# FNet mixing and SwiGLU: folding the first batch crosswise, set by set, and fetching its weights behind x

## The chip, the cores and the metric

The kernel runs on one core of a Trainium2 chip. The metric is the device time of one execution in microseconds (us). One execution was also recorded by the hardware profiler. All times below are from those runs and from that profile.

## The reference

`x` has 8 batches of 3008 rows by 256 columns, in float32. Each batch goes through a Fourier transform over rows and one over columns, and the real part is kept. The 24064 rows then go through a SwiGLU block with 1536 hidden columns.

```python
def _attn_ref(x):
    X = np.fft.fft(x, axis=1)
    X = np.fft.fft(X, axis=2)
    return X.real.astype(np.float32)

def _moe_ref(x, w_gate, w_val, w_out):
    g = x @ w_gate
    silu = g * (1.0 / (1.0 + np.exp(-g)))
    val = x @ w_val
    return (silu * val @ w_out).astype(np.float32)
```

## The kernel before

**What is computed where.** The column transform is folded into the weights: `Wp` and `Wq` are the gate and value weights multiplied by tables of cosines (`CD`) and sines (`SDt`), and `Wm` is `Wq` times -2 but for one row. The row transform is a matmul with a table of cosines and sines, `Tab`. Its length is cut by symmetry: the rows of a batch are cut into four quarters of 752 rows; rising rows of a quarter are added to falling rows of another (a sum and a difference), and the columns of the result are folded once more, the upper half reversed onto the lower. What is left are two sets of rows, set A with 128 rows (buffer `XA`) and set C with 60 rows of each half (buffer `XC`; batch 0 uses `XC0`). The matmuls with `Tab` give, for each batch, a sum part and a difference part, from which additions and subtractions on VectorE write the tiles `Pt` and `Qt` of 480 or 512 columns. These are the inputs of the feed-forward part.

**The main loop.** For each tile there are 12 units of 128 hidden columns. A unit is a matmul for the gate and one for the value, from `Pt` with `Wp` and from `Qt` with `Wq` or `Wm` (line 1337); then a Silu on ScalarE (line 1372 in the first units, later 1449, 1472, 1521, 1524), a product on VectorE or GpSimd (1375, 1540, 1548, 1551), and a matmul with `Wo` (line 1601). A planner written in the kernel sets the order in which these and the work for the next batches are issued. The scheduled work of the first tile also holds the transform of the remaining weight columns (lines 1808 to 1823), which come from `Wraw`, and the fetch of `Wo` (line 1974).

**The prologue.** Everything ahead of the main loop is written out by hand, and each engine runs its instructions in the order in which they are written. All of the change lies here.

- Lines 264 to 274: the fetches of x for batch 0. Rising rows of set A come in one DMA, falling ones in four, two of them issued by ScalarE. Set C comes in two rises (`rise_c`, line 270) and four falls (`fall_c`, line 273). Line 277 clears half of `XC0` on ScalarE first. SP's DMAs use eight semaphores in turn, and one that takes a semaphore again waits for the landing of the one that had it.
- Lines 356 to 411: small tables, and `row_signs`, on GpSimd. Line 363 (`turns`) and line 367 (`angles`) make the angles for `Tab`; lines 374, 377, 383 and 386 are the sines, cosines, negated copies and the weighing of `Tab` on ScalarE. `load_w` fetches the first 512 columns of the two weights (line 394, tiles `W0`) and the others (line 396, `Wraw`, which lies in the memory of `XA` and so waits until set A has been read).
- Line 444 (`place`): a matmul with a permutation brings the rising rows into the order of the falling ones.
- Line 453 (`sums`): sums and differences of the placed rows and the falling ones, for set A into `SA` and for set C into `SC`, 128 x 512 each, on VectorE.
- Line 511 (`fold_d`): the columns of set A folded, on GpSimd, into `EOA` in float32; line 512 casts that to `EOb` on ScalarE. Line 507 (`fold_c`) folds set C on VectorE into bfloat16.
- Lines 497 and 503 (`half_folded`, `folded_c`): the matmuls with `Tab`. Line 611 (`row0`): the column 0 that the fold leaves out, as matmuls with one row of output; its operands come from `heads` (lines 457, 458, GpSimd).
- Line 473 (`half_w`): the first weights times `CD` or `SDt`, in halves of 256 columns with gate and value in one PSUM bank; the copies out of PSUM are lines 475 (ScalarE) and 477 (VectorE), and line 481 (`double`) writes `Wm`.
- Line 642 copies the one part of the product to SBUF (`od`), and line 647 (`put`) writes `Pt` and then `Qt` from it on VectorE.
- Line 668: two entries of the operand `BBc` of batch 0 (`St`). Line 669 clears a piece of `Af`, and line 671 is two DMAs of SP that write these zeros into the unused partitions of `XC`. The same queue of SP then holds the loads of batch 1: set C (lines 166, 168, 175), a copy inside `XC` (line 180), and set A (lines 151, 153). The folds of batch 1 run on GpSimd (lines 189 to 213).

Of the kernel before, what the change touches and what calls it, by code (L numbers as in the profile page):

```python
# [17 lines left out]

@with_exitstack
def kernel(
# [27 lines left out]

# [12 lines left out]

# [55 lines left out]

# [147 lines left out]
    nc.scalar.copy(xf[:, 4 * D:8 * D], zero.to_broadcast([P, 4 * D]))  # L277
# [39 lines left out]

# [148 lines left out]

    def half_w(h, k, pool, nm):
        ps = pool.tile([P, 2, T // 2], F32, name=nm)
        dst, tab = ((Wp, CD), (Wq, SDt))[k]
        fs = slice(h * T // 2, (h + 1) * T // 2)  # L470
        for gv in range(2):
            for no in range(2):
                nc.tensor.matmul(ps[:, gv, :], tab[:, no, :], W0[gv][:, no, fs], start=(no == 0), stop=(no == 1))
        if k or not h:
            nc.scalar.copy(dst[:, :, fs], ps)
        else:
            nc.vector.tensor_copy(dst[:, :, fs], ps)

    def double(h):
        fs = slice(h * T // 2, (h + 1) * T // 2)  # L480
        nc.scalar.activation(Wm[:, :, fs], Wq[:, :, fs], AF.Copy, scale=m2)
# [33 lines left out]
    def transform_w(fc, gv, k, ps):  # L515
        dst, tab = ((Wp, CD), (Wq, SDt))[k]
        src = W0[gv] if fc == 0 else Wraw[gv][:, :, (fc - 1) * T:fc * T]
        fs = slice(fc * T, (fc + 1) * T)
        for no in range(2):
            nc.tensor.matmul(ps, tab[:, no, :], src[:, no, :], start=(no == 0), stop=(no == 1))  # L520

        def copies():
            if k:
                nc.scalar.copy(dst[:, gv, fs], ps)
                if fc == 1:
                    nc.scalar.activation(Wm[:, gv, fs], ps, AF.Copy, scale=m2)
                else:
                    pts(Wm[:, gv, fs], dst[:, gv, fs], scalar1=m2, scalar2=1.0, op0=Alu.mult, op1=Alu.mult)
            else:
                nc.vector.tensor_copy(dst[:, gv, fs], ps)  # L530
        return copies

    def first_rows():
        ps = psO.tile([P, T], F32, name="o")
        for gv in range(2):
            for f in range(nF):
                nc.tensor.matmul(ps[:, gv * nF + f:gv * nF + f + 1], Wq[0:1, gv, f * P:(f + 1) * P], sel[0:1, 0:1],
                                 start=True, stop=True)
        nc.scalar.copy(w0.rearrange("p g f -> p (g f)"), ps[:, 0:2 * nF])

# [22 lines left out]
    for k, a in ((0, 0), (1, 0), (0, 1)):  # L563
        sums(SC, k, XC0, psC, (a,))
# [1466 lines left out]
```

## Time and profile before

| | |
|---|---|
| median of 3 runs | 600.81 us (600.59 to 600.97) |
| the profiled execution, span | 599.1 us (1.7 below the median of the runs) |
| TensorE busy | 589.5 us, 98% |
| VectorE busy | 572.4 us, 96% |
| ScalarE busy | 562.6 us, 94% |
| GpSimd busy | 515.5 us, 86% |
| granted TensorE clock from 2 us to 82 us | 1.00 |

In the profile PE is TensorE, PEld its weight loads, DVE VectorE, ACT ScalarE, POOL GpSimd and SP SyncE, which issues DMAs; SPq, POOLq and PEldq are the instructions of an engine's own queue, DMA issues and waits among them. A row of the timeline gives the start, the duration, the engine, the line, what is written from what, the count, and in brackets the idle time of the engine ahead of it with what ended that. A row that stands for several instructions (x2) gives the time from the first start to the last end.

### The profile page before, as it was taken

The page shows a single profiled execution, that of the slowest core. Times are in us where ns is not written, and L with a number is a line of the kernel's source. Part 1 is how long each engine was busy: PE and PEld are TensorE (multiplying, and loading weights), DVE is VectorE, ACT ScalarE, POOL GpSimd, SP SyncE. Part 2 cuts the span into 40 slices and gives each one's busy share as a digit, 9 for nine tenths or more (in the row PEclk, how much of TensorE's full clock was granted, in tenths as well). Part 3 has the DMA queues.
Part 4 walks back from the last instruction along what each step waited for, and adds up shares of the span by engine and source line. Part 5 has one row for each costly group of instructions (what it writes and reads, how often), then busy time and mean ns, then how long its engine had stood idle before and what let it go on. Part 6 is the DMA issues. An engine that isn't in the chain of part 4 may idle for free.

```text
span 599.1 us, 12479 instructions
## 1 busy us (share of the span) xinstructions
PE 589.5 (98%) x3968; PEld 391.7 (65%) x4027; DVE 572.4 (96%) x1058; ACT 562.6 (94%) x1090; POOL 515.5 (86%) x464
## 2 busy tenths in 40 slices
PE   8999999999999999999999999999999999999997
PEld 6556666666666666566666666666666666666676
DVE  8989998999999999999999999999999999999993
ACT  8899999999989999899999999998999999999995
POOL 9828999999799999999999988997899557787772
PEclk9999999999999999999999999999999999999999
DMA  9846347344816314354245112046121211111112
GB/s 243 145 101 138 115 117 189 86 131 117 173 60 138 108 55 126 108 128 140 63 91 149 36 45 82 19 123 166 51 62 37 63 47 54 54 47 46 59 54 80
DMA packets 50556, 57.66 MB, mean 96 GB/s; under 512 B 7268, under 2 KB 37400, under 8 KB 50490
## 3 DMA queue, kind: packets, MB, share of 16 engines
q1 hardware_dynamic: 47449, 53.91, 33.7%
q0 software_dynamic: 2672, 2.36, 2.7%
q8 instruction: 31, 0.51, 0.3%
q10 hardware_dynamic: 368, 0.59, 0.3%
q14 instruction: 36, 0.29, 0.2%
HBM read 29.43 MB, written 24.65 MB: 90 GB/s over the span
## 4 chain that ended last, share of the span: by engine, by line
PE 85%; DVE 5%; ACT 3%; DMA 3%; issue 2%; POOL 2%; SPq 0%; POOLq 0%; ACTq 0%; DVEq 0%
PE o L1601 37%; PE g L1337 23%; PE v L1337 19%; PE g L1760 2%; PE o L1760 2%; DVE sv L1540 2%; DMA XA<-in_x_dram 1%; DMA XA<-in_moe_w_gate_dram 1%; DVE hp L1551 1%; DVE es L1474 1%; ACT sv L1524 1%; PE v L1601 1%; POOL hm L1548 1%; ACT v L1410 1%; PE o L1808 1%
## 5 line engine op out<-in xcount | busy, mean ns | idle before, releaser
L1548 POOL TENSOR_TENSOR hm<-sv 128x1024 bf16<-128x1024 f32 (+2 forms) x137 | 254.9, 1862 | 49.4 <-DVE sv L1540 21.5
L1540 DVE SCALAR_TENSOR_TENSOR sv<-es,v 128x512 f32<-128x512 f32 (+2 forms) x262 | 174.2, 669 | 7.4 <-PE v L1337 5.2
L1601 PE MATMUL o<-Wo,hm 128*128 128x256 bf16 (+1 forms) x1128 | 163.2, 273 | 0.4
L1601 PE MATMUL o<-Wo,hp 128*128 128x256 bf16 (+1 forms) x1104 | 159.3, 272 | 0.5
L1551 DVE TENSOR_TENSOR hp<-sp,v 128x512 bf16<-128x512 f32 (+2 forms) x236 | 157.0, 669 | 2.1 <-PE v L1337 1.4
L1601 PEld LDWEIGHTS <-hm 128*128 128x128 bf16 (+2 forms) x1140 | 111.8, 98 | 57.3 <-issue 1.1
L1601 PEld LDWEIGHTS <-hp 128*128 128x128 bf16 (+2 forms) x1140 | 111.9, 98 | 54.9 <-issue 1.5
L1524 ACT ACTIVATE sv<-g 128x512 f32<-128x512 f32 (+2 forms) x178 | 118.1, 674 | 4.2 <-PE g L1337 2.3
L1449 ACT ACTIVATE sp<-g 128x512 f32<-128x512 f32 (+2 forms) x178 | 111.1, 625 | 4.8 <-PE g L1337 1.3
L1410 ACT ACTIVATE v<-bc,w 128x512 f32<-128x512 bf16 (+2 forms) x147 | 105.7, 721 | 1.0 <-DVE hp L1551 0.6
L1337 PE MATMUL v<-Pt,Wp 128*128 128x512 bf16 (+2 forms) x287 | 106.0, 375 | 0.5
L1337 PE MATMUL g<-Pt,Wp 128*128 128x512 bf16 (+2 forms) x281 | 104.9, 374 | 0.2
L1472 ACT ACTIVATE es<-v 128x512 f32<-128x512 f32 (+2 forms) x147 | 90.7, 622 | 4.3 <-PE v L1337 2.2
L1474 DVE SCALAR_TENSOR_TENSOR es<-bc,w,v 128x512 f32<-128x512 bf16 (+2 forms) x127 | 92.9, 734 | 1.4 <-PE g L1337 0.4
L1337 PE MATMUL g<-Qt,Wq 128*128 128x512 bf16 (+2 forms) x247 | 90.4, 374 | 0.7
L1337 PEld LDWEIGHTS <-Wp 128*128 128x128 bf16 x576 | 56.3, 98 | 27.2 <-issue 0.8
L1337 PE MATMUL g<-Qt,Wm 128*128 128x512 bf16 (+2 forms) x187 | 70.3, 376 | 0.3
L1453 DVE SCALAR_TENSOR_TENSOR sg<-bc,w,g 128x512 f32<-128x512 bf16 (+2 forms) x96 | 69.2, 721 | 0.3 <-PE g L1337 0.2
L1524 ACT ACTIVATE sv<-sg 128x512 f32<-128x512 f32 (+2 forms) x96 | 66.5, 697 | 0.4 <-DVE sg L1517 0.4
L1521 ACT ACTIVATE sp<-g 128x512 f32<-128x512 f32 (+2 forms) x96 | 59.2, 616 | 5.9 <-DVE sg L1517 5.5
L1517 DVE SCALAR_TENSOR_TENSOR sg<-sg,g 128x512 f32<-128x512 f32 (+2 forms) x96 | 63.4, 660 | 0.5
L1337 PEld LDWEIGHTS <-Wq 128*128 128x128 bf16 x429 | 41.9, 98 | 26.9 <-issue 0.7
(196 smaller groups left out, 777.3 us busy)
## 6 DMA issues: line engine op xcount, KB each, us to landing
out_dram<-ev SPq DMA_DIRECT2D x96, 128.0 KB
XA<-in_x_dram SPq DMA_DIRECT2D x30, 256.0 KB
XA<-in_x_dram SPq DMA_DIRECT2D x112, 64.0 KB
XC<-in_x_dram SPq DMA_DIRECT2D x28, 120.0 KB
XC<-in_x_dram SPq DMA_DIRECT2D x105, 32.0 KB
bc<-br SPq DMA_DIRECT2D x19, 128.0 KB
St<-Fc SPq DMA_DIRECT2D x12, 128.5 KB
out_dram<-ev SPq DMA_DIRECT2D x12, 120.0 KB
```

The costliest lines, as they stand in the source:

```text
L1337: nc.tensor.matmul(ps[:, :n], Wt[:, gv, fs], src[:, :n], start=start, stop=stop, skip_group_check=True)
L1410: nc.scalar.activation(T_[kv][:, :w], bc[t][:, :w], AF.Copy, scale=w0[:, 1, f:f + 1])
L1449: nc.scalar.activation(sp_to()[:, :w], T_[kg][:, :w], AF.Silu)
L1453: nc.vector.scalar_tensor_tensor(T_[keg][:, :w], bc[t][:, :w], w0[:, 0, f:f + 1], T_[kg][:, :w], op0=Alu.mult, op1=Alu.add)
L1472: nc.scalar.activation(T_[kes][:, :w], T_[kv][:, :w], AF.Copy, scale=2.0 if on_pool(u) > 1 else 1.0)
L1474: nc.vector.scalar_tensor_tensor(T_[kes][:, :w], bc[t][:, :w], w0[:, 1, f:f + 1], T_[kv][:, :w], op0=Alu.mult, op1=Alu.add)
L1517: nc.vector.scalar_tensor_tensor(T_[kgm][:, :w], T_[keg][:, :w], 2.0, T_[kg][:, :w], op0=Alu.mult, op1=Alu.subtract)
L1524: nc.scalar.activation(sv()[:, f % 2, w - 1::-1, 1], T_[kgm if by_dve else kg][:, :w], AF.Silu)
L1540: nc.vector.scalar_tensor_tensor(sv()[:, f % 2, w - 1::-1, 0], T_[kes][:, :w], 2.0, T_[kv][:, :w], op0=Alu.mult, op1=Alu.subtract)
L1548: nc.gpsimd.tensor_tensor(hts_(t)[1][:, f - 1:f + 1, :w], sv()[:, :, :w, 1], sv()[:, :, :w, 0], op=Alu.mult)
L1551: nc.vector.tensor_tensor(hts_(t)[0][:, f, :wp], T_[ksp][:, :wp], T_[kv][:, :wp], op=Alu.mult)
L1601: nc.tensor.matmul(st["ps"][:n, j, :], hts[t][minus][:, f, c:c + n], Wo[:, f, :], start=(f == 0), stop=(f == nF - 1))
```

## The change

The first batch's sums are no longer made twice. One pass on VectorE adds the placed rows and the falling rows with their columns reversed (`cross`, 255 columns of each half), and the sum and the difference are both made from this one result, from its two halves (`halves`). The column that has no partner is added by itself (`ends`). This is done set by set. Two of the four folds of set A are written a second time on VectorE straight into bfloat16 (`fold_b`); the other two are cast on ScalarE as before (`half_cast`). The four folds on GpSimd stay, and the latter two stand later. `row0` takes six operands for each half, copied into `ENb`, where it took four, and uses the whole width of the table.

The order of the prologue changes with it. Both rises of set C are issued ahead of the falls, and the falls behind a clearing of half of `XC0`, now on GpSimd. The first weights are fetched behind the first fold on GpSimd, and the weights of the later columns ahead of the last two folds. `half_w` becomes `first_w`, 512 columns of one weight at a time, gate first. The additions that write tile 0, `Pt` then `Qt`, come ahead of those of tile 1. The clearing of `Af` and with it SP's two zero puts stand behind both doublings, and `row_signs` at the end. The four groups of warm matmuls have 12 in place of 13. Functions that nothing called are removed (not shown), and the sizes of two spacers in memory change.

```diff
     EOA = tq.tile([P, 2, 4, 2, P + 1], F32, name="EOA")
-    SC = tq.tile([P, 2, 2, 2, D], F32, name="SC")
-    SA = tp.tile([P, 2, 4, 2, D], F32, name="SA")
     EOb = tp.tile([P, 2, 4, 2, P], BF16, name="EOb")
     XC0 = tp.tile([P, 4, 2, D], F32, name="XC0")
...
+    FA = tp.tile([P, 4, 2, D], F32, name="FA")
+    FC = tp.tile([P, 2, 2, D], F32, name="FC")
+    Ec0 = tp.tile([P, 2, 2, 1], F32, name="Ec0")
+    ENb = tp.tile([P, 6, 2, 1], BF16, name="ENb")
...
     fall_a(3, nc.scalar)
-    nc.scalar.copy(xf[:, 4 * D:8 * D], zero.to_broadcast([P, 4 * D]))
     fall_a(2, q)
     fall_a(1, nc.scalar)
     fall_a(0, q)
     for a in range(2):
         rise_c(a, q)
-        fall_c(1, a, q)
-        fall_c(0, a, q)
...
-        for j in range(13):
+        for j in range(12):
...
     turns(ti[0], kf, 0)
+    turns(ti[1], kf, 1)
     more_iotas()
-    turns(ti[1], kf, 1)
+    nc.gpsimd.memset(xf[:, 4 * D:8 * D], 0.0)
+    for a in range(2):
+        fall_c(1, a, q)
+        fall_c(0, a, q)
     nc.gpsimd.dma_start(out=XC0[NCR:64 + NCR + 1:64, 2:4, 0],
                         in_=rows_at(0, 0, [[2 * R * D, 2], [R * D, 2], [1, D]]))
     pts(putC, putC, scalar1=pcol, scalar2=1.0, op0=Alu.is_equal, op1=Alu.mult)
     nc.gpsimd.memset(EOf[:, 1, :, P:P + 1], 0.0)
     nc.gpsimd.memset(sel[0:1, :], 1.0)
-    row_signs()
-    load_w(1, (0,))
...
     sine(1, 0, NCE, ce_angle[1][0])
+    cosine(1, 0, NCE, ce_angle[1][1])
+    weigh_ce()
     opposite(0)
-    nc.scalar.activation(ce_angle[1][1], ce_angle[1][0], AF.Abs, bias=zero)
...
-    def sums(S, k, X, pss, only=None):
-        n = len(pss)
-        for a in only or range(n):
-            down = X[:, 7 - a] if n == 4 else X[:, 2 + a]
-            vtt(S[:, k, a], pss[a], down[:, ::-1, :], op=(Alu.add, Alu.subtract)[k])
...
+    def cross(F, X, pss, a):
+        down = X[:, 7 - a] if len(pss) == 4 else X[:, 2 + a]
+        vtt(F[:, a, :, 1:D], pss[a][:, :, 1:D], down[:, ::-1, D - 1:0:-1], op=Alu.add)
+    def ends(to, X, pss, a):
+        down = X[:, 7 - a] if len(pss) == 4 else X[:, 2 + a]
+        vtt(to, pss[a][:, :, 0:1], down[:, ::-1, 0:1], op=Alu.add)
+    def halves(F, a0, n):
+        return F[:, a0:a0 + n, :, P:0:-1], F[:, a0:a0 + n, :, P:D]
+    SUMS = (Alu.add, Alu.subtract)
...
-    def half_w(h, k, pool, nm):
-        ps = pool.tile([P, 2, T // 2], F32, name=nm)
-        dst, tab = ((Wp, CD), (Wq, SDt))[k]
-        fs = slice(h * T // 2, (h + 1) * T // 2)
-        for gv in range(2):
-            for no in range(2):
-                nc.tensor.matmul(ps[:, gv, :], tab[:, no, :], W0[gv][:, no, fs], start=(no == 0), stop=(no == 1))
-        if k or not h:
-            nc.scalar.copy(dst[:, :, fs], ps)
-        else:
-            nc.vector.tensor_copy(dst[:, :, fs], ps)
-    def double(h):
-        fs = slice(h * T // 2, (h + 1) * T // 2)
-        nc.scalar.activation(Wm[:, :, fs], Wq[:, :, fs], AF.Copy, scale=m2)
...
-    def folded_c(eo, qs=(0, 1)):
-        for a in range(2):
-            for q in qs:
-                dst, rhs = set_cols(acc[eo][q], Tab[:, 1, q, eo], a)
-                nc.tensor.matmul(dst, EB[:, eo, a, q, :], rhs, start=False, stop=a == 1, skip_group_check=True)
-    def fold_c(eo):
-        s_ = SC[:, eo]
-        vtt(EB[:, eo], s_[:, :, :, P:0:-1], s_[:, :, :, P:D], op=(Alu.add, Alu.subtract)[eo])
+    def folded_c(eo, a):
+        for q in range(2):
+            dst, rhs = set_cols(acc[eo][q], Tab[:, 1, q, eo], a)
+            nc.tensor.matmul(dst, EB[:, eo, a, q, :], rhs, start=False, stop=a == 1, skip_group_check=True)
+    def fold_c(eo, a):
+        r_, f_ = halves(FC, a, 1)
+        vtt(EB[:, eo, a:a + 1], r_, f_, op=SUMS[eo])
     def fold_d(eo, a0):
-        s_ = SA[:, eo, a0:a0 + 2]
-        ptt(EOA[:, eo, a0:a0 + 2, :, 0:P], s_[:, :, :, P:0:-1], s_[:, :, :, P:D], op=(Alu.add, Alu.subtract)[eo])
+        r_, f_ = halves(FA, a0, 2)
+        ptt(EOA[:, eo, a0:a0 + 2, :, 0:P], r_, f_, op=SUMS[eo])
+    def half_cast(eo, a0):
         nc.scalar.copy(EOb[:, eo, a0:a0 + 2], EOA[:, eo, a0:a0 + 2, :, 0:P])
+    def fold_b(eo, a0):
+        r_, f_ = halves(FA, a0, 2)
+        vtt(EOb[:, eo, a0:a0 + 2], r_, f_, op=SUMS[eo])
...
+    def first_w(gv, k, by):
         dst, tab = ((Wp, CD), (Wq, SDt))[k]
+        ps = psO.tile([P, T], F32, name="o")
         for no in range(2):
+            nc.tensor.matmul(ps, tab[:, no, :], W0[gv][:, no, :], start=(no == 0), stop=(no == 1))
+        def copy():
+            (nc.scalar.copy if by else nc.vector.tensor_copy)(dst[:, gv, 0:T], ps)
+        return copy
+    def double(gv):
+        nc.scalar.activation(Wm[:, gv, 0:T], Wq[:, gv, 0:T], AF.Copy, scale=m2)
...
-    sums(SA, 0, XA, psA, (0, 1))
-    sums(SA, 1, XA, psA, (0, 1))
-    sums(SA, 0, XA, psA, (2, 3))
-    sums(SA, 1, XA, psA, (2, 3))
+    for a in range(2):
+        cross(FA, XA, psA, a)
+    for a in range(2):
+        ends(EOA[:, 0, a, :, P:P + 1], XA, psA, a)
+    start_acc(0)
     start_acc(1)
-    start_acc(0)
     fold_d(0, 0)
-    cosine(1, 0, NCE, ce_angle[1][1])
-    half_folded(0, 0)
-    psC = place(XC0, putC, 2, ((psO, "o"),))
+    load_w(1, (0,))
     fold_d(1, 0)
     load_w(1, (1,))
-    weigh_ce()
+    for a in range(2, 4):
+        cross(FA, XA, psA, a)
+    for a in range(2, 4):
+        ends(EOA[:, 0, a, :, P:P + 1], XA, psA, a)
+    load_w(0)
+    psC = place(XC0, putC, 2, ((psO, "o"),))
+    half_cast(0, 0)
+    opposite(1)
+    half_cast(1, 0)
+    fold_b(0, 2)
+    fold_b(1, 2)
+    half_folded(0, 0)
+    half_folded(0, 2)
     half_folded(1, 0)
+    half_folded(1, 2)
+    cross(FC, XC0, psC, 0)
+    fold_c(0, 0)
+    folded_c(0, 0)
+    cross(FC, XC0, psC, 1)
+    fold_c(0, 1)
+    folded_c(0, 1)
+    fold_c(1, 0)
+    fold_c(1, 1)
+    for a in range(2):
+        ends(Ec0[:, a], XC0, psC, a)
+    nc.vector.tensor_copy(ENb[:, 0:4], EOA[:, 0, :, :, P:P + 1])
+    nc.vector.tensor_copy(ENb[:, 4:6], Ec0)
+    copies = [first_w(0, 0, 1), first_w(0, 1, 0)]
+    for a in range(2):
+        folded_c(1, a)
     fold_d(0, 2)
     fold_d(1, 2)
-    load_w(0)
-    opposite(1)
-    half_folded(0, 2)
-    half_folded(1, 2)
-    for k, a in ((0, 0), (1, 0), (0, 1)):
-        sums(SC, k, XC0, psC, (a,))
-    fold_c(0)
-    sums(SC, 1, XC0, psC, (1,))
-    fold_c(1)
-    X3c = XC.rearrange("p a q d -> p (a q d)")
-    hd = tp.tile([P, 2, 2, 1], F32, name="hd")
-    ptt(hd, SA[:, 0, 0:2, :, 0:1], SA[:, 0, 2:4, :, 0:1], op=Alu.add)
-    heads(nc.gpsimd, hd[:, 0], hd[:, 1], CEa)
-    heads(nc.gpsimd, SC[:, 0, 0, :, 0:1], SC[:, 0, 1, :, 0:1], CEc)
     nc.gpsimd.iota(kfO, pattern=[[4, G]], base=1, **iota)
     turns(rrO[:, 0].bitcast(I32), kfO, 0)
...
-        todo = [(CE[:, q, 0, k, P:P + 1], Tab[:, 0, q, 0, e], e) for k, e in ((0, E0), (1, E1))]
-        todo += [(CEc[:, q, 0, k, 0:1], Tab[:, 1, q, 0, e], e) for k, e in ((0, E0), (1, E1))]
-        for l, r_, cols in todo:
-            nc.tensor.matmul(ps[0:1, cols], l, r_, start=False, stop=True, skip_group_check=True)
+        for k in range(6):
+            dst, rhs = set_cols(ps[0:1], Tab[:, k // 4, q, 0], k % 4)
+            nc.tensor.matmul(dst, ENb[:, k, q, :], rhs, start=False, stop=True, skip_group_check=True)
...
+    def even_copy(eo):
+        od = odp.tile([P, NCE], F32, name="od")
+        nc.scalar.copy(od, acc[eo][0][:, 0:NCE])
+        return od
+    def first_puts(eo, od, tiles):
+        for c0, s0, minus in ((0, 1, 0), (GH, 0, 1), (G, GH + 1, 0), (G + GH, GH + 1, 1)):
+            for t, off, src, w in pieces(c0, GH):
+                if t in tiles:
+                    s_ = slice(s0 + src, s0 + src + w)
+                    vtt(pq_tiles(t)[eo][:, off:off + w], acc[eo][1][:, s_], od[:, s_], op=SUMS[minus])
+        if 1 in tiles:
+            vtt(last[eo][:, 0:1], acc[eo][1][:, 0:1], od[:, 0:1], op=Alu.add)
...
+    copies[0]()
+    copies[1]()
+    od0 = even_copy(0)
+    for i in range(2):
+        row0(0, i, acc[1][i])
+    od1 = even_copy(1)
+    first_puts(0, od0, (0,))
+    first_puts(1, od1, (0,))
+    copies = [first_w(1, 0, 1), first_w(1, 1, 1)]
+    copies[0]()
+    copies[1]()
+    first_puts(0, od0, (1,))
+    first_puts(1, od1, (1,))
+    angles(rrO[:, 0], kfO, 0, rrO[:, 0].bitcast(I32), (0,))
+    double(0)
+    double(1)
     for k in range(2):
-        nc.scalar.activation(BBc[:, :, 1, k, 0:1], SC[:, 0, 1 - k, :, 0:1], AF.Copy, scale=(nsgn, sgn)[k])
+        nc.scalar.activation(BBc[:, :, 1, k, 0:1], Ec0[:, 1 - k], AF.Copy, scale=(nsgn, sgn)[k])
     nc.scalar.copy(zeros, zero.to_broadcast([P, D]))
     for hi in range(2):
         q.dma_start(out=X3c[64 * hi + NCR:64 * hi + 64, :].rearrange("p (c d) -> p c d", d=D),
                     in_=zeros[64 * hi + NCR:64 * hi + 64].unsqueeze(1).to_broadcast([64 - NCR, 16, D]))
-    folded_c(0)
-    transform(0, 0, (0,), acc)
-    angles(rrO[:, 0], kfO, 0, rrO[:, 0].bitcast(I32), (0,))
-    for k in range(2):
-        half_w(0, k, psO, "o")
-    for i in range(2):
-        folded_c(1, (i,))
-        row0(0, i, acc[1][i])
-    transform(0, 0, (1,), acc)
-    double(0)
-    for k in range(2):
-        half_w(1, k, psO, "o")
-    double(1)
+    row_signs()
```

More of the change, by code (lines that the diff above doesn't have):

```diff
@@ L411 @@
     nc.gpsimd.memset(sel[0:1, :], 1.0)
-    row_signs()
-    load_w(1, (0,))
     ce_angle = [[tp.tile([P, 2, NCE], F32, name=f"{nm}{ch}") for nm in ("rr", "ra")] for ch in range(2)]
-    tp.tile([P, 2924], F32, name="pad")
+    tp.tile([P, 3900], F32, name="pad")
     angles(ce_angle[0][0], kf, 0, ti[0])
     magnitude(ce_angle[0][1], ce_angle[0][0])
+    vts(putA, putA, scalar1=pcol, scalar2=None, op0=Alu.is_equal)
     angles(ce_angle[1][0], kf, 1, ti[1])
+    magnitude(ce_angle[1][1], ce_angle[1][0])
     nc.vector.memset(Tab[:, :, :, :, NOO - 1:NOO], 0.0)
@@ L516, in transform_w @@
+    def first_w(gv, k, by):
         dst, tab = ((Wp, CD), (Wq, SDt))[k]
-        src = W0[gv] if fc == 0 else Wraw[gv][:, :, (fc - 1) * T:fc * T]
-        fs = slice(fc * T, (fc + 1) * T)
+        ps = psO.tile([P, T], F32, name="o")
         for no in range(2):
[L520 to L539, printed above, removed]
+            nc.tensor.matmul(ps, tab[:, no, :], W0[gv][:, no, :], start=(no == 0), stop=(no == 1))
@@ L601, in row0 @@
     def row0(b, q, ps):
-        CE = coef_a(b)[0]
         if b:
@@ L621, in products @@
         return res + [(BBc[:, q, eo, k, :], Tab[:, 1, q, (eo + k) % 2, NOO:NTAB], slice(0, G)) for k in range(2)]
-    def transform(b, part, eos, given=None):
-        n = NCE if part == 0 else G
-        ev, ods = {}, {}
-        for q, pool, nm in ((0, psO, "o"), (1, psG, "g")):
-            if given:
-                ps = {eo: given[eo][q] for eo in eos}
-            else:
-                ps = {eo: pool.tile([P, T], F32, name=nm) for eo in eos}
-                for eo in eos:
-                    mms = products(b, part, q, eo)
-                    for i, (l, r_, cols) in enumerate(mms):
-                        nc.tensor.matmul(ps[eo][:, cols], l, r_, start=(i == 0), stop=(i == len(mms) - 1),
-                                         skip_group_check=True)
-            if part == 0 and 1 in eos and not given:
-                row0(b, q, ps[1])
-            for eo in eos:
-                if q == 0:
-                    ods[eo] = odp.tile([P, NCE], F32, name="od")
-                    nc.scalar.copy(ods[eo][:, 0:n], ps[eo][:, 0:n])
-                else:
-                    ev[eo] = ps[eo]
-        def put(eo, dst, s0, w, minus):
-            nc.vector.tensor_tensor(dst, ev[eo][:, s0:s0 + w], ods[eo][:, s0:s0 + w],
-                                    op=Alu.subtract if minus else Alu.add)
-        if part == 0:
-            runs = [(0, GH, 1, 0), (GH, GH, 0, 1), (G, GH, GH + 1, 0), (G + GH, GH, GH + 1, 1)]
-        else:
-            runs = [(2 * G, G, 0, 0), (3 * G, G, 0, 1)]
-        todo = []
-        for eo in eos:
-            for c0, n_, s0, minus in runs:
-                for t, off, src, w in pieces(b * H + c0, n_):
-                    todo.append((t, eo, off, s0 + src, w, minus))
-        for t, eo, off, s0, w, minus in sorted(todo, key=lambda v: v[0:2]):
-            put(eo, pq_tiles(t)[eo][:, off:off + w], s0, w, minus)
-        if part == 0:
-            for eo in eos:
-                put(eo, last[eo][:, b:b + 1], 0, 1, 0)
```

10 lines of the change are left out of this document (3 added, 7 removed).

## The prediction

> **What bounds the kernel now.** I read the page's busy times first, then the chain that ended last, then the timeline of the first 24 us, where all of the edit lies (from the first matmul of the main loop on, the instructions of every engine stand in the same order as before).
>
> ```profile
> PE 589.5 (98%) x3968; PEld 391.7 (65%) x4027; DVE 572.4 (96%) x1058; ACT 562.6 (94%) x1090; POOL 515.5 (86%) x464
> PE 85%; DVE 5%; ACT 3%; DMA 3%; issue 2%; POOL 2%; SPq 0%; POOLq 0%; ACTq 0%; DVEq 0%
> ```
>
> PE is busy for 589.5 of 599.1 us, so the main loop has next to no air. What the change can move is the time at which that loop gets going, and whether something that feeds it later comes late. The timeline (start, us, engine, line, operation, idle time and releaser) shows how it gets going:
>
> ```profile
> 16.12 0.39 ACT L669 COPY Af<-zero 128x256 f32<-128x256 f32 x1
> 16.53 1.48 SPq L671 DMA_DIRECT2D XC<-Af  x2
> ...
> 17.09 0.58 ACT L475 CAST Wp<-o 128x512 bf16<-128x512 f32 x1
> ...
> 17.74 0.33 PE L611 MATMUL v<-Tab,CEa 128*1 128x189 bf16 x2
> ...
> 18.64 0.72 ACT L481 ACTIVATE Wm<-Wq,m 128x512 bf16<-128x512 bf16 x1
> ...
> 19.90 0.37 PE L1337 MATMUL g<-Pt,Wp 128*128 128x480 bf16 x1
> ...
> 21.13 0.39 PE L1808 MATMUL o<-XA,CD 128*128 128x512 bf16 x1 [0.26 <-DMA XA<-in_moe_w_gate_dram]
> ...
> 22.02 1.03 ACT L1372 ACTIVATE sg<-g 128x480 f32<-128x480 f32 x2 [0.59 <-PE g L1337]
> ...
> 22.82 0.37 PE L1337 MATMUL g<-Qt,Wm 128*128 128x480 bf16 x1
> ...
> 23.42 1.10 POOL L1974 DMA_DIRECT2D Wo<-in_moe_w_out_dram  x1
> ```
>
> The first loop matmul comes at 19.90, the first weights of the later columns (L1808) make PE wait until 21.13, the first Silu (L1372) starts at 22.02, and the first matmul into a reused slot (`g<-Qt,Wm`) 0.80 later. After that PE is dense (59.11 of the 59.50 us from 22.8 to 82.3). A second line of work starts here: the zeros copied at 16.12 go out by two puts (L671), and behind these in SP's queue stand all loads of batch 1.
>
> ```profile
> 24.89 1.79 SPq L166 DMA_DIRECT2D XC<-in_x_dram  x2
> ...
> 31.18 0.65 SPq L168 DMA_DIRECT2D XC<-in_x_dram  x1
> ...
> 39.03 0.90 SPq L180 DMA_DIRECT2D XC<-XC  x1
> 40.10 1.52 SPq L151 DMA_DIRECT2D XA<-in_x_dram  x4
> ```
> ```profile
> 57.24 1.89 POOL L1548 TENSOR_TENSOR hm<-sv 128x1024 bf16<-128x1024 f32 x1 [1.48 <-DMA out_dram<-ev]
> 59.09 2.36 POOL L189 TENSOR_TENSOR SDf<-XA 128x1020 f32<-128x1020 f32 x1
> ```
> ```profile
> L189 POOLq EVENT_SEMAPHORE  x9: 17/43/1237, 40.1 to 58.7; - x9
> ```
> ```profile
> 81.41 0.65 ACT L1524 ACTIVATE sv<-g 128x512 f32<-128x512 f32 x1 [0.32 <-POOL hm L1548]
> ...
> 82.28 0.38 PE L1337 MATMUL g<-Pt,Wp 128*128 128x512 bf16 x1
> ```
>
> The fold of batch 1 (POOL, 59.09) reads those loads. Its waits on their landings (the semaphore row of its line: count, shortest, median and longest ns, first and last start) end at 58.7: 0.4 us of slack. From 59.09 to 81.40 POOL is busy for 22.15 of 22.31 us, so it can't catch up, and at 81.41 ACT already waits for its `hm`. That ACT row ends at 82.06 and the matmul that overwrites its `g` starts at 82.28: 0.2 more. So a chain of loads that is late by c costs c minus 0.6, and PE, having no air, keeps the loss.
>
> **The change, part by part.**
>
> *Sums and folds.* 12 sums of 0.69 (L453) become 6 cross passes of about 0.69; with 4 casting folds on DVE (two of 0.69 for set A, and set C in four of half the size, about 0.43 each) and 8 small copies and adds at about 0.2 the DVE work falls from 12 x 0.6 + 2 x 0.69 = 8.6 to 6 x 0.6 + 2 x 0.69 + 4 x 0.43 + 8 x 0.2 = 8.3, which in itself is nothing. But the last cross pass now waits only for the placing of set C, and 2 ACT casts (0.62 each) go. POOL keeps its four folds of 1.09; the last two move behind both weight fetches and lose their reader on the critical path.
>
> *PE from the last piece of x on.* The first batch is 8 + 2 + 2 pieces, 3.1 MB; the window 2 to 10 us moved 314 GB/s. The second rise is now issued about 2.7 us earlier (before at 5.96), behind 2.1 + 0.5 MB: 2 + 2.62/0.314 = 10.3 at best, 11.9 if everything has to be in; I take 11.1. From there PE has: placing 0.86 (two L444 starts), 16 half folds at 0.16 (four L497 take 0.64) 2.56, set C even 0.64, gate weights 4 x 0.215 = 0.86, set C odd 0.64, row 0 as 12 matmuls of 377 columns at 0.16 = 1.92 (before 8 of 189 at 0.08 = 0.66, plus 0.96 of issue gaps), value weights 0.86. Sum 8.34: 19.4. The first weights go out about 10.4 instead of 8.15 and took 4.0 and 5.4 us to land, so 14.4 to 15.8 against a need at 15.2: up to 0.6, I take 0.3. First loop matmul 19.7, as before (19.90) within its error of about 0.5.
>
> *Later weights.* Their fetch (L396, before 14.39, 6.70 us on the way) moves up by some 1.6 us; the wait in front of L1808 (0.73 on the weight load) is then no longer the last. Alone that would give up to 0.7.
>
> *ACT's tail.* What is late next is ACT: after the value matmuls, at about 19.5, it has two copies (0.5 each), two doublings (start to start 0.61), two St entries (0.18) and the zeros (0.37), together 2.95, then the Silu: 22.45 against 22.02. So the loop starts late by m = +0.4, between 0 and 0.9. (Before, three of these, 0.75, were done at 16.12 under other waits.)
>
> *The zeros and SP's queue.* The copy of zeros moves from 16.12 to the end of that tail, about 22.1, so the puts (L671) start at 22.4 in place of 16.53: 5.9 late. They have nothing else to hide behind: all 24 loads of set C of batch 1, then the copy at 39.03, then the 20 loads of set A stand behind them. What survives of 5.9 at the copy: the issue rows between 18.06 and 39.03 add up to 17.2, less 2.3 in two that hold a wait, and gaps of 0.05 make 15.6, so with no wait at all 22.4 + 1.5 + 15.6 = 39.5: c = +0.5 at least. At most all: +5.9. Between them lies the fetch of Wo (issued at 23.42, 11.9 us on the way): while it ran, from 24.89 to 35.2, SP got 15 loads out, 0.69 each; in the worst stretch, 24.89 to 31.18, 8 loads, 0.79 each; without a wait 15.6 / 24 = 0.65. Before, the first six loads were ahead of it; now all stand beside or behind it. From 23.9 to 35.3 at 0.69 that is 16.5 loads and 7.5 x 0.65 behind them: 40.2, c = +1.15; at 0.79, 14.4 loads and 9.6 x 0.65: 41.5, c = +2.5. I take the middle, +1.8. Loss 1.8 - 0.6 = 1.2, which swallows m (the same PE air, not a second one). The first fold (43.43) would be 1.8 later as well, but 1.48 + 0.63 of POOL idle before 59.09 takes that up.
>
> *Small ones.* The memset on POOL (1024 wide, for the 1.03 on ACT) and the later falls of set C: 0 to 0.5, under x's own landing. The tile-0 puts first: before, `Pt` of tile 0 was ready at 19.90 and PE waited for other things; 0 to -0.3, counted as 0 since ACT decides. A warm matmul less: nothing.
>
> *A rule against it.* Two turns (L363) took 1.15 us at 2.06 and 1.63 at 3.87, beside L353 and L367 on DVE: 0.48 lost in 1.4 us of overlap. The Trainium skill (SBUF — State Buffer, "SBUF: two separate sides") says that a DVE operation with two SBUF inputs and a GpSimd operation that reads SBUF hold one port pair in turn, the loser blocked for the whole instruction. The new folds on DVE read two SBUF inputs beside POOL's 1.09 folds. By the rule up to 1.09 would be added to one DVE fold, by the row 0.5; both would lie under PE's 2.56 of half folds, unless x is early.
>
> *How Wo and the loads share.* The rows above show neither a stop nor a free run. The Trainium skill (DMA: Bandwidth & Descriptors, "Queues, rings and completion order") says that each DMA engine goes round the queues that have work, a packet at a time; by that the loads are slowed and not held up, as the rows have it, and a c of +5.9 would be left out.
>
> **Sum.** Against the profiled execution: 599.1 + 1.2 = 600.3 of span; the runs' median, 600.81, is 1.7 above the span, so 602.0.
>
> **The rivals.**
> 1. *The loads catch up* (c of 0.5 to 1.0): only ACT's tail is left, +0.4, 601.2. For it: the issue rows alone allow 39.5. Against: two waits already in that stretch.
> 2. *The whole shift survives* (c of 4 to 5.9): +3.4 to +5.3, about 605. For it: eight loads were in flight when SP stopped at 31.18, so landing and not issue can set the pace. Against: 0.69 each while Wo ran.
> 3. *Faster.* One mechanism: x is complete early. Nothing but x is on the queues until it is in (the first weights no longer share from 8.15), so the second rise lands near 10.0; PE's 8.34 then ends at 18.4, the Silu starts at 21.2 behind the same tail, `g<-Qt,Wm` at about 21.5: -1.3, 599.5. It decides if the second rise lands before about 10.3 and the loads' c stays under 0.6; the zeros then go out at 21.1, and c falls by 1.3 as well. Against: 314 GB/s is all that was moved with x alone.
> 4. *The change doesn't do what it says* (the first weights arrive late and PE waits again): +0.6 on m, 601.8, which is inside the first case.
>
> **Chances.** Forecast and rival 4 together .50 (own range 601.2 to 603.2, from c of 1.1 to 3.0; .30 of it past the bound of 0.2%, 1.2 us, which is about what runs can tell from no change), rival 1 .14 (no change), rival 2 .16, rival 3 .20 (.15 past the bound). Faster .15, same .39, slower .46. The range reaches into both ends: 599.4 leaves out about half of rival 3, 604.3 some two thirds of rival 2.
>
> **What would show it.** SP's zero puts near 22.4; the copy of XC at about 40.8; POOL's second fold of batch 1 near 60.3, with idle time in front of it that a landing ends, and ACT's wait for `hm` near 82 longer by 1 to 2. PE's row 0 near 1.9 us; no wait for the later gate weights in front of L1808's successor; the first Silu near 22.4 and `g<-Qt,Wm` near 23.2. I am wrong if the copy starts before 39.9, or if the Silu starts before 21.8 or after 23.2, or if a difference arises after 82 us that these don't explain.

## The result, and the profile after

The changed kernel takes 606.68 us (median; 605.93 to 607.25), the kernel before in the same comparison 600.89: a ratio of 1.0097, with a 95% interval of 1.0083 to 1.0112. It is 5.8 us slower. The direction was forecast, the size was not: 602.0 was predicted, with a range up to 604.3. The profiled execution has a span of 604.4 against 599.1.

The page of the changed kernel, busy times and the chain that ended last:

```profile
PE 594.4 (98%) x4019; PEld 390.6 (65%) x4019; DVE 575.4 (95%) x1065; ACT 559.9 (93%) x1086; POOL 514.1 (85%) x459
PE 82%; POOL 4%; DMA 3%; DVE 3%; issue 2%; ACT 1%; SPq 0%; POOLq 0%; ACTq 0%; DVEq 0%
```

PE is as dense as before, so the loss is a later start or a wait. POOL, 2% of the chain before, now has 4%. The timeline of the prologue:

```profile
11.22 3.89 DVE L484 TENSOR_TENSOR EOb<-FA 128x512 bf16<-128x512 f32 x2
11.41 1.10 POOL L477 TENSOR_TENSOR EOA<-FA 128x512 f32<-128x512 f32 x1
...
13.67 1.08 PEld L464 LDWEIGHTS <-EOb 128*128 128x128 bf16 x8 [0.75 <-DVE EOb L484]
...
15.04 0.68 DVE L432 TENSOR_TENSOR FC<-o,XC 128x510 f32<-128x510 f32 x1
...
16.39 0.11 PEld L469 LDWEIGHTS <-EOf 128*128 128x128 bf16 x2 [0.79 <-DVE EOf L473]
...
17.62 0.11 PEld L469 LDWEIGHTS <-EOf 128*128 128x128 bf16 x2 [1.11 <-DVE EOf L473]
...
18.36 0.11 PEld L490 LDWEIGHTS <-CD 128*128 128x128 bf16 x2 [0.63 <-DVE Ec L436]
...
19.98 1.12 PE L580 MATMUL v<-Tab,ENb 128*1 128x377 bf16 x6
...
22.87 0.37 PE L1280 MATMUL g<-Pt,Wp 128*128 128x480 bf16 x1
...
25.21 0.39 ACT L626 COPY Af<-zero 128x256 f32<-128x256 f32 x1
...
25.50 1.03 ACT L1315 ACTIVATE sg<-g 128x480 f32<-128x480 f32 x2
```

Two folds on VectorE (L484) take 3.89 us, where L507 took 0.69 for one of the same size. The first pass over set C (L432) therefore starts at 15.04, PE's weight loads wait for VectorE five times (four are shown, the fifth is 0.42 at 15.17), and the gate weights are made at 18.36. The first loop matmul comes at 22.87 (before 19.90), the first Silu at 25.50 (before 22.02), 3.48 late. Then the loads, first SP's queue and then POOL's folds of batch 1:

```profile
25.62 1.49 SPq L628 DMA_DIRECT2D XC<-Af  x2
27.16 1.44 SPq L151 DMA_DIRECT2D XC<-in_x_dram  x2
28.64 2.92 SPq L160 DMA_DIRECT2D XC<-in_x_dram  x1
...
35.20 0.87 SPq L160 DMA_DIRECT2D XC<-in_x_dram  x1
...
45.66 0.90 SPq L165 DMA_DIRECT2D XC<-XC  x1
```
```profile
61.66 1.89 POOL L1491 TENSOR_TENSOR hm<-sv 128x1024 bf16<-128x1024 f32 x1
64.70 2.36 POOL L174 TENSOR_TENSOR SDf<-XA 128x1020 f32<-128x1020 f32 x1 [1.15 <-DMA XA<-in_x_dram]
```
```profile
87.00 0.64 ACT L1467 ACTIVATE sv<-g 128x512 f32<-128x512 f32 x1 [1.08 <-POOL hm L1491]
```

The puts are 9.09 late, the copy of XC 6.63, and POOL's second fold of batch 1 is 5.61 late and now waits 1.15 for a landing. ScalarE's wait for `hm`, 0.32 at 81.41 in the kernel before, is 1.08 at 87.00. Set against the same ScalarE instructions of the kernel before (by the times of that kernel), lateness is 3.5 at the first Silu, 3.35 from 30 to 53 us, 3.95 near 56, 4.85 near 66, 5.6 from 83 to 160, and 5.3 at the end. So some 3.3 us are lost before the loop and 2.3 more by 83 us; 0.3 come back later.

### The profile page after: what moved, and what is told of

It reads as the page before. It is cut to its first block, busy times and chain, and to the rows that moved or that the text cites. A ratio compares the mean times of both kernels' runs of the same rounds, so it can differ in the third digit from the quotient of the medians.

```text
span 604.4 us, 12522 instructions
## 1 busy us (share of the span) xinstructions
PE 594.4 (98%) x4019; PEld 390.6 (65%) x4019; DVE 575.4 (95%) x1065; ACT 559.9 (93%) x1086; POOL 514.1 (85%) x459
## 4 chain that ended last, share of the span: by engine, by line
PE 82%; POOL 4%; DMA 3%; DVE 3%; issue 2%; ACT 1%; SPq 0%; POOLq 0%; ACTq 0%; DVEq 0%
PE o L1544 35%; PE g L1280 23%; PE v L1280 18%; DMA XA<-in_x_dram 3%; PE g L1703 2%; PE o L1703 2%; POOL hm L1491 2%; DVE sv L1483 1%; POOL SDf L174 1%; DVE hp L1494 1%; DVE es L1417 1%; PE v L1544 1%; PE o L1751 0%; PE o L575 0%; PE g L575 0%
## 5 line engine op out<-in xcount | busy, mean ns | idle before, releaser
L1483 DVE SCALAR_TENSOR_TENSOR sv<-es,v 128x512 f32<-128x512 f32 (+2 forms) x262 | 176.0, 676 | 8.8 <-PE v L1280 5.8
L1494 DVE TENSOR_TENSOR hp<-sp,v 128x512 bf16<-128x512 f32 (+2 forms) x236 | 158.8, 677 | 2.2 <-PE v L1280 1.3
L1280 PE MATMUL g<-Pt,Wp 128*128 128x512 bf16 (+2 forms) x288 | 107.5, 374 | 1.5 <-ACT sv L1467 1.5
L1280 PE MATMUL g<-Qt,Wq 128*128 128x512 bf16 (+2 forms) x288 | 104.6, 375 | 0.0
L1280 PE MATMUL g<-Qt,Wm 128*128 128x512 bf16 (+2 forms) x192 | 72.1, 376 | 0.5 <-ACT sg L1315 0.5
```

The lines of the kernel that those rows point to most:

```text
L1280: nc.tensor.matmul(ps[:, :n], Wt[:, gv, fs], src[:, :n], start=start, stop=stop, skip_group_check=True)
L1483: nc.vector.scalar_tensor_tensor(sv()[:, f % 2, w - 1::-1, 0], T_[kes][:, :w], 2.0, T_[kv][:, :w], op0=Alu.mult, op1=Alu.subtract)
L1494: nc.vector.tensor_tensor(hts_(t)[0][:, f, :wp], T_[ksp][:, :wp], T_[kv][:, :wp], op=Alu.mult)
```

## The experiments

The table gives medians, the ratio to the kernel before with its 95% interval, and three starts in the profile: the first Silu, the copy inside XC, and POOL's second fold of batch 1.

| kernel | us | ratio | Silu | copy | fold |
|---|---|---|---|---|---|
| before | 600.5 to 600.9 | 1 | 22.02 | 39.03 | 59.09 |
| changed | 606.68 | 1.0097 [1.0083, 1.0112] | 25.50 | 45.66 | 64.70 |
| a_zeros_early | 603.97 | 1.0053 [1.0038, 1.0068] | 25.42 | 38.50 | 62.38 |
| b_zeros_late | 604.73 | 1.0066 [1.0051, 1.0081] | 21.54 | 43.12 | 62.62 |
| a_dma_behind | 607.77 | 1.0119 [1.0102, 1.0135] | 25.97 | 46.77 | 65.73 |
| a_fold_behind | 609.05 | 1.0132 [1.0117, 1.0148] | 28.09 | 48.08 | 67.21 |
| a_narrow_zeros | 602.65 | 1.0034 [1.0021, 1.0047] | 24.13 | 38.32 | 61.09 |
| a_quiet_zeros | 605.05 | 1.0070 [1.0053, 1.0086] | 25.64 | 36.59 | 63.13 |
| a_quiet_zeros_narrow | 606.99 | 1.0103 [1.0088, 1.0118] | 26.33 | 37.39 | 64.62 |
| best1 | 606.59 | 1.0097 [1.0082, 1.0112] | 27.63 | 38.51 | 65.75 |
| a_quiet2_zeros | 602.99 | 1.0040 [1.0025, 1.0055] | 23.22 | 37.88 | 60.98 |
| best2 | 602.05 | 1.0023 [1.0014, 1.0033] | 22.13 | 38.49 | 60.24 |
| best3 | 600.88 | 1.0006 [0.9997, 1.0015] | 21.72 | 38.38 | 59.24 |
| b_wraw_early | 601.04 | 1.0006 [0.9997, 1.0015] | 22.13 | 38.43 | 59.08 |

### The late zeros, undone and done alone

In the changed kernel, the zeros moved up:

```diff
     half_cast(1, 0)
+    nc.scalar.copy(zeros, zero.to_broadcast([P, D]))
+    for hi in range(2):
+        q.dma_start(out=X3c[64 * hi + NCR:64 * hi + 64, :]...
     fold_b(0, 2)
...
-    nc.scalar.copy(zeros, zero.to_broadcast([P, D]))
-    for hi in range(2):
-        q.dma_start(out=X3c[64 * hi + NCR:64 * hi + 64, :]...
```

> The changed kernel with the clearing of Af and SP's two zero puts moved up behind the second cast of set A (near 13 us, where ACT is idle). Theory L (the late zeros delay the loads of batch 1, and that adds a loss of its own to the late start of the loop): the puts go out by 14, the copy of XC comes at 39 or before, POOL's second fold of batch 1 near 61 instead of 64.7, and only the late start is left: the first Silu at about 25.1 (25.50 less the 0.37 of the copy on ACT), 3.1 late, so about 604.0. Rival L0 (the loads are hidden and the late start alone makes the whole loss): 606.3, the fold still near 64.

Measured: 603.97, 2.7 less than the changed kernel. The copy comes at 38.50, the fold no longer waits for a landing, and only the late start is left. In the kernel before, the same six lines moved behind `double(1)`:

> The kernel before, with only the clearing of Af and the two zero puts moved behind both doublings. Theory L: the puts start near 22.2, 5.7 late; in the changed kernel 6.63 of 9.09 us survived at the copy of XC, 0.73 of it, so here the copy comes at about 43.2, and the end is 4.1 - 0.6 = 3.5 later: 604.4. The blind estimate of what survives (1.2 to 2.5) would give 601.4 to 602.7. Rival L0: only the 0.4 on ACT, 601.2.

Measured: 604.73, 4.0 slower than the kernel before in the same comparison (600.70). Its own SP queue and POOL:

```profile
21.48 1.48 SPq L684 DMA_DIRECT2D XC<-Af  x2
23.01 4.39 SPq L166 DMA_DIRECT2D XC<-in_x_dram  x2
...
32.59 0.87 SPq L175 DMA_DIRECT2D XC<-in_x_dram  x1
...
43.12 0.90 SPq L180 DMA_DIRECT2D XC<-XC  x1
```
```profile
62.62 2.36 POOL L189 TENSOR_TENSOR SDf<-XA 128x1020 f32<-128x1020 f32 x1 [1.62 <-DMA XA<-in_x_dram]
```

The Silu is even 0.5 early here, so nothing but the loads is late: 4.95 at the puts, 4.09 at the copy, 3.53 at the fold, 3.5 in the span (602.6 against 599.1). The rule of the prediction, c minus 0.6, gives 3.5. The first two loads take 4.39 us to issue and the first eight 1.2 each; from 32.59 on, 16 loads go out in 10.1 us, 0.63 each, which is the pace without waits. Counted load by load against the kernel before, the first is 4.95 late, the ninth 5.6 and the copy 4.09: the first ten microseconds make up for nothing, and the rest for 1.5. The fetch of Wo (from 23.1, 13.0 us on the way in this run) is under way in both stretches; what held the first eight loads is not shown.

### What held VectorE's folds

In the changed kernel, first POOL's DMA issues moved away from the two folds, then POOL's fold. Both use a small addition on POOL (`pgate`) that waits for VectorE's last fold of set A.

```diff
     fold_d(1, 0)
-    load_w(1, (1,))
...
-    load_w(0)
     psC = place(XC0, putC, 2, ((psO, "o"),))
...
     fold_b(1, 2)
+    ptt(pgate, EOb[:, 1, 3, 1, 0:1], EOb[:, 1, 3, 1, 0:1], op=Alu.add)
+    load_w(1, (1,))
+    load_w(0)
```

> The changed kernel with the issue of the value weights' fetch and of both fetches of the later weights moved behind VectorE's two folds (one small addition on POOL waits for them); POOL's fold (1,0) stays beside them. Theory P2 (POOL's folds and also its DMA issues block a DVE fold that reads two SBUF operands): the first DVE fold still waits for POOL's fold, until 12.5, and ends at 13.2; the second takes 0.69, and the first pass over set C starts at 13.9 instead of 15.04: Silu 1.1 earlier, 605.5. Theory P1 (only POOL's folds block) and rival R (a fold on DVE takes 1.6 to 2.4 us by itself): the second fold still takes 1.5 or more, pass over set C at 15.0, 606.5.

```diff
-    fold_d(1, 0)
     load_w(1, (1,))
...
-    half_cast(1, 0)
+    fold_b(1, 0)
     fold_b(0, 2)
     fold_b(1, 2)
+    ptt(pgate, EOb[:, 1, 3, 1, 0:1], EOb[:, 1, 3, 1, 0:1], op=Alu.add)
+    fold_d(1, 0)
```

> The changed kernel with POOL's fold (1,0) moved behind VectorE's folds and its result for the matmuls made by a third fold on VectorE; POOL's four DMA issues stay early, beside the three DVE folds. P1: the three take 0.69 each, from 11.2 to 13.3, and the pass over set C starts at 13.3, 1.7 earlier: 605. P2: the issues block them (0.73 each from 11.4 to 13.6), the three end near 14.5 to 15.5: 606 to 607. R: three of 1.6 to 2.4, ending at 16 to 18, and 608 or more.

Both became slower (607.77 and 609.05), and yet they answer the question. The rows of the folds on VectorE by source line (count, then shortest, median and longest in ns), first of a_dma_behind, then of a_fold_behind, and the timeline of the latter:

```profile
L485 DVE TENSOR_TENSOR EOb<-FA x2: 679/1259/1839, 11.2 to 13.0; 128x512 bf16<-128x512 f32 x2
```
```profile
L485 DVE TENSOR_TENSOR EOb<-FA x3: 680/684/684, 11.2 to 12.4; 128x512 bf16<-128x512 f32 x3
L474 DVE TENSOR_TENSOR EOf<-FC x4: 411/571/3420, 13.8 to 18.5; 128x256 bf16<-128x256 f32 x4
```
```profile
13.70 3.18 POOL L478 TENSOR_TENSOR EOA<-FA 128x512 f32<-128x512 f32 x3
13.75 3.42 DVE L474 TENSOR_TENSOR EOf<-FC 128x256 bf16<-128x256 f32 x1
```

The first fold of set A starts at 11.2 in all three kernels, under POOL's issue of the first gate weights. In the changed kernel and in a_dma_behind POOL's next instruction, at 11.41, is a fold, and VectorE's takes 2.40 and 1.84; in a_fold_behind it is another issue (11.39), and three folds on VectorE take 0.68 each beside three DMA issues of POOL. Rival R is out. But then POOL starts three folds in a row at 13.70, VectorE's half-size fold comes 0.05 later, and it ends after all three, at 17.17: 3.42 us for work of 0.41. In a_dma_behind the first fold waits for POOL's (1.84) and the second, alone, takes 0.68; there the wait has only moved, to set C's folds beside POOL's last two. So POOL's folds block VectorE's, and a start 0.18 ahead of POOL's, as in a_dma_behind, did not protect VectorE's. Part of the time of a_fold_behind has another cause: after PE's waits for set C (1.54, 0.57 and 0.55) the granted clock is 0.50 from 20.0 to 23.4 us. The part on the DMA issues stays open: VectorE's two folds took 2.40 and 1.57 with the issues directly behind POOL's fold, 1.84 and 0.68 without them, but 0.68 each beside issues alone. The last 0.5 of the 1.57 also lies beside POOL's next fold (from 14.61, itself 1.45 in place of 1.09).

That is the Trainium skill's rule (SBUF — State Buffer, "Who interferes with whom"), that a DVE instruction with two SBUF inputs contends with a GpSimd instruction that reads SBUF, and these runs agree with it; a wait through three instructions is more than the whole of one, which that section speaks of. It was not so each time: in best1 (below) two additions of two columns on VectorE, 0.16 each in best2, started beside the first and the second of POOL's three folds and took 1.09 and 1.06, one fold each.

### Row 0, and both folds kept apart

Row 0 as 8 narrow matmuls, with the zeros early (shown is how their operands are made):

```diff
-    nc.vector.tensor_copy(ENb[:, 0:4], EOA[:, 0, :, :, P:P + 1])
-    nc.vector.tensor_copy(ENb[:, 4:6], Ec0)
+    vtt(hd, EOA[:, 0, 0:2, :, P:P + 1], EOA[:, 0, 2:4, :, P:P + 1], op=Alu.add)
+    for k in range(2):
+        vtt(CEa[:, :, 0, k, -1:], hd[:, 0], hd[:, 1], op=SUMS[k])
+        vtt(CEc[:, :, 0, k, -1:], Ec0[:, 0], Ec0[:, 1], op=SUMS[k])
```

> The changed kernel with the zeros early and with row 0 as in the kernel before: 8 matmuls of 188 or 189 columns (their operands made by five small operations on VectorE in place of two copies). If row 0 lies on the path (it stands between the gate and the value weights on PE, and ACT's tail follows the latter): 1.0 to 1.2 us off, Silu near 24.3, 602.9. If ACT's or VectorE's other work hides it: 603.9.

Measured: 602.65, 1.3 less than a_zeros_early; the Silu 1.29 earlier. Row 0 lies on the path with its full length.

Then POOL's folds held back until VectorE's last fold is done (what the next two kernels add to this is told in their expectations):

```diff
-    fold_d(1, 0)
-    load_w(1, (1,))
...
-    load_w(0)
...
-    half_cast(1, 0)
...
+    fold_b(1, 0)
     fold_b(0, 2)
     fold_b(1, 2)
+    ptt(pgate, EOb[:, 1, 3, 1, 0:1], EOb[:, 1, 3, 1, 0:1], op=Alu.add)
+    load_w(1, (1,))
+    load_w(0)
...
     fold_c(1, 1)
+    ptt(pgate, EB[:, 1, 1, 1, 0:1], EB[:, 1, 1, 1, 0:1], op=Alu.add)
+    fold_d(1, 0)
```

> The changed kernel with the zeros early, and with POOL kept from folding while VectorE folds: three folds of set A on VectorE (1,0 too), then the fetches of the value weights and of the later weights, and POOL's folds (1,0), (0,2), (1,2) only when the last fold of set C is done (two small additions on POOL wait for VectorE). Theory P (VectorE's folds with two SBUF operands are blocked while POOL folds, and that made the loop late): every DVE fold takes 0.4 to 0.7, the last ends near 16.0, the gate weights are made at 16.3 in place of 18.4, the first Silu comes near 22.7 and the time is 603.97 - 2.7 = 601.3. Rival X (the late falls of x or the late first weights hold the start): the Silu stays at 24.5 or later, 603 or more.

> Both of the above together. If each lies on the same path in series: 603.97 - 2.7 - 1.1 = 600.2, Silu near 21.6, about the kernel before. If the one hides the other: 601.3.

> Both of the above, and ACT's tail shortened: the two entries of St ahead of the first weight copies, and the gate's doubling between the two copies of od, where ACT is idle. If ACT's tail sets the start of the loop as forecast, the Silu comes 0.9 earlier again, near 20.7, and the time is 599.3, 1.4 below the kernel before. If the later weights (their fetch goes out at about 14.4) or the puts on VectorE end last, 600.0 or more.

All three missed: 605.05, 606.99 and 606.59. VectorE did what was expected (every fold 0.4 to 0.7, the last ending at 15.9), but the value weights, whose fetch now left at 13.34 together with the later weights and the loads of batch 1, were 7.5 to 8.7 us on the way. They took 5.2 in the changed kernel, and 4.2 in a_dma_behind, where they left at 13.89 but the loads of batch 1 were not out yet. PE waited for them 1.20, 2.01 and 3.14 us, and then 1.69, 1.07 and 1.19 for the later gate weights, which were 10.6 to 12.0 us on the way instead of 7.0. The timeline of best1 and its windows (busy time and count of PE, PEld, DVE, ACT and POOL, then the granted clock, DMA share and GB/s):

```profile
22.13 0.60 PE L492 MATMUL o<-W,CD 128*128 128x512 bf16 x2 [3.14 <-DMA W<-in_moe_w_val_dram]
```
```profile
18.90:22.10 3.20, 0.09 (x2) 0.00 (x0) 2.74 (x14) 1.08 (x2) 2.90 (x7) 1.00 1.06 194
22.10:24.50 2.40, 2.37 (x8) 0.80 (x8) 0.58 (x1) 1.70 (x3) 2.40 (x4) 0.66 0.57 130
24.50:27.00 2.50, 1.31 (x5) 0.35 (x4) 0.00 (x0) 0.20 (x1) 2.34 (x3) 0.50 0.35 79
```

The 0.66 is the mean of a window in which the clock changed: it is 1.00 up to 22.85 and 0.50 from 22.9 to 29.7. In a_quiet_zeros_narrow it is 0.50 from 22.0 to 28.7, and in a_quiet_zeros it stays at 1.00; the two narrow kernels came out behind the one that they were to improve.

The mistake was mine: the weights' fetch stood behind the wait, though a_fold_behind had shown that it may go beside the folds. With all four issues from 10.6 on and only POOL's folds behind:

```diff
-    fold_d(1, 0)
     load_w(1, (1,))
...
-    half_cast(1, 0)
...
+    fold_b(1, 0)
...
     fold_c(1, 1)
+    ptt(pgate, EB[:, 1, 1, 1, 0:1], EB[:, 1, 1, 1, 0:1], op=Alu.add)
+    fold_d(1, 0)
```

> Like the kernel that kept POOL from folding while VectorE folds, but with POOL's four DMA issues in a row from 10.6 on (beside VectorE's folds, where a run of this study showed that they cost the folds nothing), so that the value weights are not 8.7 us on the way; POOL's folds (1,0), (0,2), (1,2) wait for the last fold of set C. Theory P: DVE's folds end near 16.0, the value weights land before 19, no wait of PE for a weight, first Silu near 22.8 against 25.4 with the zeros early alone: 603.97 - 2.6 = 601.4. Rival X (the loop is late for another reason, the later weights or x): 603 or more.

Measured: the Silu at 23.22, 2.2 earlier than with the zeros early alone (2.6 expected), and 602.99. The start of the loop behaves as theory P says. Half of the gain is given back inside the loop: lateness against the kernel before grows from 0.9 to 1.9 between 27 and 30 us, with POOL's work now some 2 us behind. Best2 shows where this bites.

> The same, with row 0 of 8 narrow matmuls (its operands made before POOL's folds begin), the entries of St and the zeros on ACT ahead of the first weight copies (near 16.5), and the gate's doubling between the two copies of od. If row 0 (1.3) and ACT's tail (0.9) come off in series: Silu near 20.8, which is 1.2 before the kernel before, and 599.6. If the later weights land last (they are behind the first on one queue and share it with the loads of batch 1): Silu after 22 and 600.8 or more.

Measured: 602.05. Its timeline:

```profile
22.13 1.03 ACT L1322 ACTIVATE sg<-g 128x480 f32<-128x480 f32 x2 [1.26 <-POOL sgo L338]
...
27.14 2.02 DVE L349 SCALAR_TENSOR_TENSOR XA<-XA,mM 128x376 f32<-128x376 f32 x2
...
29.77 0.36 PE L1287 MATMUL v<-Qt,Wm 128*128 128x480 bf16 x1 [0.40 <-DVE hp L1325]
```

The Silu waits 1.26 us for `row_signs` on POOL, and the angles on VectorE, again with two SBUF inputs and beside POOL, take 2.02 for two; `hp` and PE follow late. The first of the two stands beside POOL's issue of `Wo` and takes 1.00; in the changed kernel one beside the same issue took 0.60, so here too the part of the issues is open. Against best2, best3 takes `row_signs` and the first turns out of that queue (the lines at their later places go):

```diff
     nc.gpsimd.memset(sel[0:1, :], 1.0)
+    row_signs()
...
+    nc.gpsimd.iota(kfO, pattern=[[4, G]], base=1, **iota)
     ptt(pgate, CEc[:, 1, 0, 1, 0:1], CEc[:, 1, 0, 1, 0:1], op=Alu.add)
+    turns(rrO[:, 0].bitcast(I32), kfO, 0)
     fold_d(1, 0)
```

> The version before this one, with row_signs back at its early place (the first Silu waited 1.26 us for it) and POOL's iota and first pair of turns ahead of the three late folds. If POOL's displaced work is what held that version (the Silu by row_signs, and later VectorE's angles, which took 2.0 for two beside POOL): the Silu near 21.0 in place of 22.13 and the later loss of 1.0 partly gone: 600.0 to 600.9. If the Silu only gives way and the loss inside the loop grows by as much: 602.

Measured: 600.88 against 600.64, ratio 1.0006 [0.9997, 1.0015]: no difference that these runs can tell. With the zeros early, row 0 narrow and the folds apart the loss is gone, and the new way of folding then gives nothing: its Silu is 0.3 earlier than before, but 0.6 is lost again between 27 and 30 us, where the two angles beside POOL still take 1.99.

Last, in the kernel before, the one wait for a weight that the prediction named:

```diff
     fold_d(0, 2)
+    load_w(0, (0,))
     fold_d(1, 2)
-    load_w(0)
+    load_w(0, (1,))
```

> The kernel before, with the fetch of the later gate weights moved up by one POOL fold (1.09), between the folds (0,2) and (1,2). In the kernel before PE waits for that fetch (0.73 on the weight load) and the first Silu 0.59 for PE. If that is what sets the start of its loop: up to 0.6 off, 600.1. If the fold (1,2), 0.73 later, or ACT's doublings take its place: 600.5 to 600.9.

Measured: 601.04, no difference. PE's wait for the later gate weights is gone and the Silu is at 22.13: the later fold (1,2) and ACT's doublings took its place.

## Why the prediction was wrong

- **The step that failed first** is "both would lie under PE's 2.56 of half folds", the treatment of VectorE's folds beside POOL's. The blocking was priced at 0.5 to 1.09 for one fold and then counted as nothing. It cost 2.6 on the two folds of set A (3.89 for 1.3), and set C's passes and folds stand behind them in VectorE's queue; they had no cover, since PE's half folds wait for the same folds. PE's terms behind the placing were right in themselves (row 0: 1.92 forecast, 2.02 measured from 19.98 to the next start), but PE came to the gate weights at 18.36, where the sum gives 11.1 + 0.86 + 2.56 + 0.64 = 15.16. Of these 3.2 us, 0.5 lie ahead of the half folds (both placings of set C, 1.77, ran from 10.73, where the sum has one, 0.86, from 11.1), and 2.7 are waits for VectorE. So m was 3.48, not 0.4, and the first Silu, at 25.50, is past the 23.2 that the prediction named as a sign of being wrong. The rule that was quoted against the change was the one that decided; a_fold_behind and a_quiet2_zeros show it (2.2 of the lost 3.4 come back when POOL is quiet).
- **Row 0** was in the sum with its right length, but its cost over the narrow form was taken as 0.3, with gaps of 0.96 counted to the narrow form that the kernel before has for other reasons. Done alone it is worth 1.3.
- **The chain of loads** was right as a mechanism, place by place: puts, copy, POOL's second fold, ACT and PE, with a loss of c minus 0.6 (b_zeros_late: 3.5 by the rule and 3.5 in the span; changed kernel: 6.0 by the rule, 5.3 in the span). The term c was mis-sized, 1.8 forecast and 6.63 measured. There are two parts. The puts were 9.09 late and not 5.9, 3.2 more, carried over from m, since they stand behind ACT's tail. And the pace was taken from rows in which six loads had gone ahead of Wo: of a lateness of 5.9 the sum kept 1.8, 0.3 of it; measured were 0.73 (6.63 of 9.09) and 0.83 (4.09 of 4.95). (The 0.69 counts 15 loads from 24.89 to 35.2, where the rows have 14, 0.74 each; that alone would make c about 1.9.) So the inference that a c of 5.9 "would be left out" failed, and rival 2, the whole shift, was the nearer one. That the loads make up for nothing in their first ten microseconds is shown; why is open.
- **The later weights** ceased to be the last wait, as forecast, and that gave nothing, also as b_wraw_early shows for the kernel before.
- The size of the losses together, from a_zeros_early and a_narrow_zeros: 2.7 for the zeros, 1.3 for row 0, and a_quiet2_zeros about 1.0 at the end (2.2 at the Silu) for the blocked folds. That is 5.0 of 5.8; they are not exactly additive.

## What to carry to other kernels

When work moves to VectorE beside GpSimd, count the operands that both read from SBUF, and put the wait into the chain of what follows on VectorE's queue, not only into the one instruction. When an instruction that releases a queue (here a copy of 0.39 us with two small DMAs behind it) moves back, follow everything behind it in that queue to its last reader, and price its lateness in full unless rows show idle time in the queue itself: here 0.73 and 0.83 of it was left 20 us later, and it made 2.7 of the 5.8 us. A fix that holds an engine back must look at what that engine was to do next: here fetches, signs and turns.

## What the runs showed of the hardware

- A fold on VectorE with both operands in SBUF, started 0.05 us after the first of three back-to-back folds on POOL, ended only after all three: 3.42 us for 0.41 (a_fold_behind). Two small additions in best1 waited for one fold each (1.09 and 1.06 for 0.16). A start of VectorE 0.18 us ahead of POOL's fold did not help it (1.84 for 0.68, a_dma_behind). Three folds in a row beside POOL's DMA issues alone took 0.68 each.
- After PE had stood still for 3.1 us the granted clock was 0.50 from 22.9 to 29.7 (best1), and matmuls of 480 columns started 0.40 apart in place of 0.20. Here the wait cost more than itself. It was 0.50 for 3.4 us after waits of 1.54, 0.57 and 0.55 (a_fold_behind), and stayed at 1.00 with waits of 1.20 and 1.69 (a_quiet_zeros).
- The fetch of the 256 KB of value weights took 4.2 us in a_dma_behind and 8.7 in best1, where the loads of batch 1 were also on the queues.
